# First layer in two halves of the f-tiles over all chunks, one weight conversion per step, second layer's chunks reversed

## The chip, the cores and the metric

The kernel runs on one core of a Trainium2 chip. The metric is the device time of one execution in microseconds (us); lower is better. The kernel before took 620.69 us (median of three runs, 618.83 to 621.95).

## The reference

Attention with a learned position bias (2 batches, 8 heads, 576 positions, head size 64) gives 1152 tokens of 512 features. Two feed-forward layers follow, each 512 to 2048 to 512. Only they are touched by the change:

```python
def _moe_ref(x, w_in, w_out):
    h = x @ w_in
    g = h * (1.0 / (1.0 + np.exp(-1.702 * h)))
    return (g @ w_out).astype(np.float32)

def _moe2_ref(x, w_in, w_out, a, b):
    h = x @ w_in
    h2 = h * h
    h3 = h2 * h
    P = a[0] + a[1] * h + a[2] * h2 + a[3] * h3
    Q = 1.0 + np.abs(b[0]) * np.abs(h) + np.abs(b[1]) * h2
    g = P / (Q + 1e-06)
    return (g @ w_out).astype(np.float32)
```

The weights arrive as 64-bit floats and are turned into 32-bit ones on the chip.

## The kernel before, in words

**Order of work.** Bias and attention come first and are not touched but for the early weight fetches. The two layers are one loop of steps (line 782). The tokens are cut into three chunks of 384 (`NC`), the 2048 hidden features into 16 f-tiles of 128 (`NF`). A step n is one layer l, chunk c and f-tile k; `seq` (line 770) lists them layer by layer, chunk by chunk, f-tile by f-tile, so steps 0 to 47 are the first layer and 48 to 95 the second. Steps 0 to 2 begin under the end of attention (line 753).

**One step.** `hidden` (line 461) makes the 128 by 384 block of h on TensorE in 12 matmuls: numbers are kept as a high and a low part, so three products over four blocks of 128 features. The block is in PSUM tile `hps`, of which there are two. In the first layer `gelu` (line 483), one step later, takes the sigmoid on ScalarE (486), multiplies on VectorE (487; this is the last reader of `hps`), and `parts` splits the result into `ghi` on ScalarE (477) and `glo` on GpSimd (480). In the second layer `rational` (line 494) spreads the fraction over three successive steps on ScalarE (503 to 511), VectorE (513 to 523) and GpSimd (520, 522); line 523 is the last reader of `hps`, and line 503 squares into the fourth accumulator's tile, `acc3`.

**Second product.** `out1` (line 536) adds the f-tile's product with `w_out` into four accumulators `acc0` to `acc3` (12 matmuls), two steps behind `hidden` (`L1`); `out2` (line 543) into three (9 matmuls of 512 columns), four steps behind (`L2`). The accumulators hold a whole chunk, all 16 f-tiles, and there is one set. At a chunk's end `input2` (line 775) makes the second layer's input: ScalarE copies each accumulator to the high part (778), VectorE subtracts for the low part (779). For the last chunk this waits until step 50 (`later`, line 802). `pairs` (line 529) orders the matmuls of a chunk's first and last f-tile so that accumulators are begun late and finished early, one after the other.

**Weights.** A layer's f-tile has two halves, `w_in` and `w_out`, of 512 KB as 64-bit numbers; 64 halves in all, in the order `M.order`. `fetch` (line 413) loads one into a `raw` tile (four of them) on the SP queue. `conv(j)` (line 425) finishes half j-1 with an integer add on VectorE (440) and begins half j: ScalarE shifts the low words (444), VectorE picks bits of the high words (445, 447). In the first layer line 445 writes the PSUM tile `top`; in the second it writes the SBUF tile `tmp`. `split` (line 451) then makes the high part on ScalarE (456) and the low part on GpSimd (457) and fetches half j+3. `M.W[k]` holds f-tile k of the first layer and later of the second.

**When conversions run** (lines 787 to 799). Ten begin under attention (lines 723 to 725). The first layer's others go two per step during chunk 0, to step 14. None run in steps 15 to 32. The second layer's start when chunk 2 has used an f-tile for the last time: 26 of them in steps 33 to 47, mostly two per step, and the last six in every second step from 54 to 64.

In a step the program's order is: `hidden`; conversion and `split`; `gelu` of the step before; a possible second conversion and `split`; from step 48 on `rational`; then `out1` or `out2`, and at a chunk's end `input2`. Each engine keeps that order.

Of the kernel before, what the change touches and what calls it, by code (L numbers as in the profile page):

```python
# [4 lines left out]
F32 = mybir.dt.float32  # L5
F32R = mybir.dt.float32r
U32 = mybir.dt.uint32
I32 = mybir.dt.int32
AF = mybir.ActivationFunctionType
ALU = mybir.AluOpType  # L10
# [7 lines left out]
NF = 16  # L18
CH = 384
NC = 3  # L20
NEARLY, NMID = 3, 7

L1, L2 = 2, 4
# [375 lines left out]
class Moe:  # L399
# [13 lines left out]
    def fetch(self, j):  # L413
        if j >= 64:
            return
        nc = self.nc
        l, k, o = self.half(j)
        raw = self.rp.tile([128, 512, 2], U32, tag="raw", name="raw", bufs=4)
        src = self.t["win" if o == 0 else "wout"][l, k]
        nc.sync.dma_start(raw[:], src.bitcast(U32).rearrange("p (n t) -> p n t", t=2))  # L420
        self.raw[j] = raw
# [3 lines left out]
    def conv(self, j):  # L425
        nc = self.nc
        if j < 64:
            raw = self.raw[j]
            val = self.tmp[j] = self.rp.tile([128, 512], U32, tag="tmp", name="tmp", bufs=3)
            lo, hi = raw[:, :, 0], raw[:, :, 1]  # L430
            self.up[j], tmp = lo, val[:]
            if self.hs:
                self.up[j] = self.hs.tile([128, 512], F32, tag="up", name="up", bufs=1)[:].bitcast(U32)
                if not self.second:
                    tmp = self.hs.tile([128, 512], F32, tag="es", name="top", bufs=1)[:].bitcast(U32)
        if j:
            l, k, o = self.half(j - 1)
            w, old = self.W[k], self.tmp.pop(j - 1)
            self.raw.pop(j - 1)
            nc.vector.tensor_tensor(out=old[:].bitcast(I32), in0=old[:].bitcast(I32),  # L440
                                    in1=self.up.pop(j - 1).bitcast(I32), op=ALU.add)
            self.ready = w, o, old[:].bitcast(F32), j + 3
        if j < 64:
            nc.scalar.activation(out=self.up[j].bitcast(I32), in_=lo, func=AF.Copy, scale=2.0 ** -29)  # L444
            nc.vector.tensor_scalar(out=tmp, in0=hi, scalar1=5, scalar2=2,  # L445
                                    op0=ALU.logical_shift_left, op1=ALU.logical_shift_right)
            nc.vector.scalar_tensor_tensor(out=val[:], in0=hi, scalar=0xC0000000, in1=tmp,  # L447
                                           op0=ALU.bitwise_and, op1=ALU.bitwise_or)
# [45 lines left out]
    def rational(self, h):  # L494
        nc, ab = self.nc, self.ab
        t2, t1, t0 = self.st[1], self.st[0], None
        vec, act = nc.vector, nc.scalar.activation
        if h is not None:
            t0 = [(self.mp if i else self.gp).tile([128, CH], F32, tag=f"t{i}", name="ra", bufs=3) for i in range(3)]
        self.st = [t0, t1]  # L500
        if t2:
            sq = self.ps.tile([128, 512], F32, tag="acc3", name="sq", bufs=1)[:, 0:CH]
            act(out=sq, in_=t2[0][:], func=AF.Square, bias=self.neg)
        if t1:
            es = self.hs.tile([128, 512], F32, tag="es", name="es", bufs=1)[:, 0:CH]
            act(out=t1[1][:], in_=t1[0][:], func=AF.Abs_reciprocal_sqrt)  # L506
            act(out=es, in_=t1[1][:], func=AF.Square)
        if t0:
            act(out=t0[0][:], in_=h, func=AF.Square)  # L509
            act(out=t0[1][:], in_=h, func=AF.Abs, scale=ab[:, 4:5])  # L510
            act(out=t0[2][:], in_=h, func=AF.Identity, scale=ab[:, 3:4], bias=ab[:, 2:3])  # L511
        if t2:
            vec.scalar_tensor_tensor(out=t2[2][:], in0=sq, scalar=0.75, in1=t2[2][:], op0=ALU.add, op1=ALU.mult)
        if t1:
            vec.tensor_tensor(out=t1[0][:], in0=es, in1=t1[0][:], op=ALU.mult)
            vec.scalar_tensor_tensor(out=t1[2][:], in0=t1[2][:], scalar=ab[:, 0:1], in1=es,
                                     op0=ALU.add, op1=ALU.mult)
        if t0:
            vec.tensor_tensor(out=t0[2][:], in0=t0[2][:], in1=h, op=ALU.mult)  # L519
            nc.gpsimd.tensor_scalar(out=t0[0][:], in0=t0[0][:], scalar1=self.pb[:, 1:2], scalar2=1.000001,  # L520
                                    op0=ALU.mult, op1=ALU.add)
            nc.gpsimd.tensor_tensor(out=t0[0][:], in0=t0[0][:], in1=t0[1][:], op=ALU.add)  # L522
            vec.scalar_tensor_tensor(out=t0[2][:], in0=t0[2][:], scalar=ab[:, 1:2], in1=h,  # L523
                                     op0=ALU.add, op1=ALU.mult)
        if t2:
            return self.parts(t2[2][:], 0)


    def pairs(self, k, n):
        if k == 0:  # L530
            return [(i, e) for e in range(n) for i in range(3)]
        if k == NF - 1:
            return [(0, 0), (1, 0), (0, 1), (1, 1), (2, 0), (2, 1)] + [(i, e) for e in range(2, n) for i in range(3)]
        return [(i, e) for i in range(3) for e in range(n)]

    def out1(self, k, g, acc):
        nc, w = self.nc, self.W[k]
        for i, e in self.pairs(k, 4):
            wi, gi = ((2, 0), (3, 0), (2, 1))[i]
            nc.tensor.matmul(acc[e][:, 0:CH], w[:, wi, 128 * e:128 * e + 128], g[gi][:],  # L540
                             start=(k == 0 and i == 0), stop=(k == NF - 1 and i == 2))

    def out2(self, k, g, acc):
        nc, w = self.nc, self.W[k]
        for i, e in self.pairs(k, 3):
            wi, gi = ((2, 0), (3, 0), (2, 1))[i]
            nc.tensor.matmul(acc[e][:], g[gi][:, 128 * e:128 * e + 128], w[:, wi, :],  # L547
                             start=(k == 0 and i == 0), stop=(k == NF - 1 and i == 2))


def attention_moe_moe(tc, t):
    nc = tc.nc
    new = tc.alloc_tile_pool
    A, M = Attention(tc, t), Moe(tc, t)
# [4 lines left out]
    op = A.op = new(name="operands", bufs=1, reuse_waits="tile")  # L559
# [27 lines left out]
    first = [(0, b, qc) for qc in QORDER for b in range(2)]  # L587
# [55 lines left out]
    for s in range(n + TLAG + 2):  # L643
# [103 lines left out]
                M.W[k] = wp.tile([128, 4, 512], F32R, name=f"w{k}")  # L747

        if s == n - 24:
            for j in range(4):  # L750
                M.fetch(j)
        if s - n in (1, 2, 3):
            hq.append(M.hidden(0, nh))
# [11 lines left out]
    for k in range(NMID, NF):  # L765
        M.W[k] = lp.tile([128, 4, 512], F32R, name=f"w{k}")

    M.st = [None, None]
    LAG = [L1, L2]
    seq = [(l, c, k) for l in range(2) for c in range(NC) for k in range(NF)]  # L770
    N1 = NC * NF
    acc, ng, later = {}, len(g), []
    todo = list(range(len(seq)))

    def input2(c, acc):
        hi, lo = M.x[c]
        for e in range(4):
            nc.scalar.copy(hi[:, e, :], acc[e][:, 0:CH])
            nc.vector.tensor_tensor(out=lo[:, e, :], in0=acc[e][:, 0:CH], in1=hi[:, e, :].bitcast(F32),
                                    op=ALU.subtract)  # L780

    for n in range(nh, len(seq) + L2):
        l, c, k = seq[n] if n < len(seq) else (2, 0, 0)
        M.second = l > 0
# [2 lines left out]
        for i in range(2):  # L787
            j = nj[0]
            if j < 33:
                go = l == 0 and c == 0  # L790
            elif j < 65:
                go = M.order[j - 1][1] + L1 * M.order[j - 1][2] < n - 32
                go = go and (n < N1 and (n, i) not in ((33, 1), (34, 1), (41, 1), (43, 0)) or n >= N1 + 6 and n % 2 == 0 and i == 0)
            else:
                go = False
            if go:
                conv(False)
            if n < N1:
                M.split()
            if i == 0 and ng <= n - 1 < N1:  # L800
                g[n - 1] = M.gelu(hq.pop(0))
        if n == N1 + 2:
            for x in later:
                input2(*x)
        if n >= N1 + RLAG:
            r = M.rational(hq.pop(0) if hq else None)
            if r:
# [2 lines left out]
        while todo and n >= todo[0] + LAG[seq[todo[0]][0]]:  # L810
            m = todo.pop(0)
            l, c, k = seq[m]
            if k == 0:
                acc = [M.ps.tile([128, 512], F32, tag=f"acc{e}", name="acc", bufs=1) for e in range(4 - l)]
            if l == 0:
                M.out1(k, g.pop(m), acc)
                if k == NF - 1:
                    if c == NC - 1:
                        later.append((c, acc))
                    else:  # L820
                        input2(c, acc)
            else:
                M.out2(k, g.pop(m), acc)
                if k == NF - 1:
                    for i in range(3):
                        o = rp.tile([128, DM], F32, tag="tmp", name="o", bufs=3)
                        rows = t["out"][CH * c + 128 * i:CH * c + 128 * i + 128, :]
                        if c < NC - 1 or i == 0:
                            nc.scalar.copy(o[:], acc[i][:])
                            nc.sync.dma_start(rows, o[:])  # L830
                        elif i == 1:
# [81 lines left out]
```

## Time and profile before

| what | value |
|---|---|
| three runs, median (lowest, highest) | 620.69 us (618.83, 621.95) |
| the profiled execution's own time | 619.0 us |
| its span, first to last instruction | 617.2 us |
| TensorE busy (matmul) | 576.5 us, 93% of the span |
| VectorE, ScalarE, GpSimd busy | 423.7, 439.4, 379.5 us |
| granted TensorE clock, mean | 0.994 |

A profile lists each engine's instructions with start and duration in us from the span's start. PE is TensorE's matmuls, PEld its weight loads, DVE VectorE, ACT ScalarE, POOL GpSimd, SP the engine that issues most DMAs. An idle time is put down to the instruction whose semaphore ended it. Matmuls are pipelined and overlap in the list, so the distance between starts tells what one costs, not its listed duration.

### The profile page before, as it was taken

What the parts mean: (1) busy time and instruction counts of PE and PEld (TensorE: products, weight loads), DVE (VectorE), ACT (ScalarE), POOL (GpSimd) and SP (SyncE); (2) the same over time, 40 slices, a digit from 0 to 9 for tenths busy, and PEclk for the clock granted to TensorE, in tenths of its full rate; (3) what the DMA queues carried; (4) which work ended last, traced back from release to release, by engine and by line L of the source; (5) the groups of instructions that cost most, each with busy time, mean ns of one, the idle gap of its engine ahead of it and who ended that gap; (6) DMA issues with size and microseconds to landing.
All of it is one profiled execution on the core that took longest, in us unless ns stands there. A gap on an engine that the chain in (4) does not pass through costs nothing.

```text
span 617.2 us, 11025 instructions
## 1 busy us (share of the span) xinstructions
PE 576.5 (93%) x3805; PEld 478.7 (78%) x3805; DVE 423.7 (69%) x918; ACT 439.4 (71%) x922; POOL 379.5 (61%) x458
## 2 busy tenths in 40 slices
PE   6987999999988998899999999988999999999997
PEld 2233466666656988899999988988988989999995
DVE  7988765888876888721113888868778766666663
ACT  7987777898886666632223666678888987788783
POOL 5967656777764677722222667756767765665663
PEclk9988999999999999999999999999999999999999
DMA  5788753836116666700001466630000100001001
GB/s 175 209 269 273 222 209 118 316 99 228 58 35 173 193 210 209 207 0 1 2 1 34 143 204 205 208 94 18 18 2 1 52 2 1 0 1 52 1 2 51
DMA packets 23912, 66.26 MB, mean 107 GB/s; under 512 B 2480, under 2 KB 3376, under 8 KB 23856
## 3 DMA queue, kind: packets, MB, share of 16 engines
q1 hardware_dynamic: 23712, 65.43, 33.3%
q8 instruction: 30, 0.49, 0.3%
q14 instruction: 26, 0.21, 0.1%
q10 hardware_dynamic: 144, 0.13, 0.1%
HBM read 52.30 MB, written 13.25 MB: 106 GB/s over the span
## 4 chain that ended last, share of the span: by engine, by line
PE 38%; DVE 14%; ACT 12%; issue 2%; POOL 0%; DVEq 0%; ACTq 0%
PE hps L468 19%; PE acc L547 13%; PE acc L540 6%; DVE tmp L440 5%; ACT up L444 3%; ACT w L456 3%; DVE sg L487 2%; DVE tmp L447 2%; DVE top L445 2%; ACT sg L486 2%; ACT ra L511 1%; ACT ra L510 1%; DVE ra L523 1%; ACT ra L506 1%; ACT ra L509 1%
## 5 line engine op out<-in xcount | busy, mean ns | idle before, releaser
L468 PE MATMUL hps<-xhi,w 128*128 128x384 f32 x768 | 152.4, 340 | 14.1 <-DVE sg L487 9.3
L468 PEld LDWEIGHTS hps<-xhi,w 128*128 128x128 f32 x768 | 135.0, 188 | 25.0 <-DVE sg L487 15.0
L457 POOL TENSOR_TENSOR w<-tmp,w 128x512 fp32r<-128x512 f32 x64 | 82.4, 1288 | 40.2 <-ACT w L456 34.1
L480 POOL TENSOR_TENSOR glo<-sg,ghi 128x384 fp32r<-128x384 f32 x48 | 48.8, 1017 | 64.4 <-PE acc L540 45.0
L468 PE MATMUL hps<-xlo,w 128*128 128x384 f32 x384 | 82.0, 334 | 0.0
L253 POOL TENSOR_SCALAR p<-p,mn 128x512 f32<-128x512 f32 x72 | 55.2, 776 | 38.6 <-ACT p L240 28.0
L540 PE MATMUL acc<-ghi,w 128*128 128x384 f32 x384 | 76.7, 334 | 0.0
L547 PE MATMUL acc<-w,ghi 128*128 128x512 f32 x288 | 75.7, 393 | 0.0
L487 DVE TENSOR_TENSOR sg<-hps,sg 128x384 f32<-128x384 f32 x48 | 26.7, 557 | 65.5 <-ACT sg L486 65.5
L240 ACT ACTIVATE p<-p,mn 128x576 f32<-128x576 f32 x72 | 55.4, 771 | 20.4 <-DVE mn L236 18.5
L520 POOL TENSOR_SCALAR ra<-ra,small 128x384 f32<-128x384 f32 x48 | 28.2, 587 | 65.9 <-ACT ra L509 65.9
L468 PEld LDWEIGHTS hps<-xlo,w 128*128 128x128 f32 x384 | 68.0, 188 | 0.0
L540 PEld LDWEIGHTS acc<-ghi,w 128*128 128x128 f32 x384 | 67.5, 188 | 0.0
L444 ACT ACTIVATE up<-raw 128x512 int32<-128x512 uint32 x59 | 37.9, 642 | 36.2 <-DVE tmp L440 33.5
L547 PEld LDWEIGHTS acc<-w,ghi 128*128 128x128 f32 x288 | 53.4, 188 | 8.6
L236 DVE CUSTOM_DVE_ANT_0 p<-wide,bt 128x576 f32<-128x576 f32 x72 | 52.2, 749 | 2.1 <-PE wide L215 1.9
L519 DVE TENSOR_TENSOR ra<-ra,hps 128x384 f32<-128x384 f32 x48 | 26.6, 554 | 36.9 <-ACT ra L511 36.8
L477 ACT CAST ghi<-sg 128x384 fp32r<-128x384 f32 x48 | 24.6, 513 | 38.2 <-DVE sg L487 19.8
L522 POOL TENSOR_TENSOR ra<-ra 128x384 f32<-128x384 f32 x48 | 48.7, 1015 | 4.0
L480 POOL TENSOR_TENSOR glo<-ra,ghi 128x384 fp32r<-128x384 f32 x48 | 48.8, 1017 | 2.4 <-PE acc L547 2.0
L215 PE MATMUL wide<-k,q 64*128 64x288 f32 (+1 forms) x432 | 45.6, 313 | 2.5 <-ACT st L142 2.0
L486 ACT ACTIVATE sg<-hps 128x384 f32<-128x384 f32 x48 | 23.4, 488 | 30.7 <-PE hps L468 30.7
(100 smaller groups left out, 1174.3 us busy)
## 6 DMA issues: line engine op xcount, KB each, us to landing
raw<-win SPq DMA_DIRECT2D x32, 512.0 KB, 3.7
raw<-wout SPq DMA_DIRECT2D x32, 512.0 KB, 3.7
bias_all<-st SPq DMA_DIRECT2D x36, 295.5 KB, 3.8
bt<-bias_all SPq DMA_DIRECT2D x16, 576.0 KB, 6.1
qk<-qk SPq DMA_DIRECT2D x7, 608.0 KB, 6.4
v<-v SPq DMA_DIRECT2D x8, 320.0 KB, 5.0
out<-o SPq DMA_DIRECT2D x8, 256.0 KB, 2.2
bt<-bias_all SPq DMA_DIRECT2D x8, 144.0 KB, 3.5
```

The costliest lines, as they stand in the source:

```text
L215: nc.tensor.matmul(ps[:, half, 0:288], q[p, x, 128 * qc:128 * qc + 128], k[p, y, 288 * half:288 * half + 288], start=(i == 0), stop=(i == ...
L236: nc.vector.tensor_tensor_reduce(out=pv.rearrange("p (x j) -> p x j", x=2), in0=ps[:, :, 0:288], in1=self.bt[qc][:, a, :].rearrange("p (x ...
L240: nc.scalar.activation(out=pv, in_=pv, func=AF.Exp, bias=mn[:, a:a + 1], scale=-1.0, accum_out=mn[:, 2 + a:3 + a])
L253: nc.gpsimd.tensor_scalar(out=p[:, a, 0:512], in0=p[:, a, 0:512], scalar1=r, scalar2=1.0, op0=ALU.mult, op1=ALU.mult)
L444: nc.scalar.activation(out=self.up[j].bitcast(I32), in_=lo, func=AF.Copy, scale=2.0 ** -29)
L457: nc.gpsimd.tensor_tensor(out=w[:, 2 * o + 1, :], in0=val, in1=w[:, 2 * o, :].bitcast(F32), op=ALU.subtract)
L468: nc.tensor.matmul(ps[:, 0:CH], w[:, wi, 128 * d:128 * d + 128], xx[:, d, :], start=(i == 0 and d == 0), stop=(i == 2 and d == 3))
L480: nc.gpsimd.tensor_tensor(out=glo[:], in0=g, in1=ghi[:].bitcast(F32), op=ALU.subtract)
L487: nc.vector.tensor_tensor(out=sg[:], in0=h, in1=sg[:], op=ALU.mult)
L522: nc.gpsimd.tensor_tensor(out=t0[0][:], in0=t0[0][:], in1=t0[1][:], op=ALU.add)
L540: nc.tensor.matmul(acc[e][:, 0:CH], w[:, wi, 128 * e:128 * e + 128], g[gi][:], start=(k == 0 and i == 0), stop=(k == NF - 1 and i == 2))
L547: nc.tensor.matmul(acc[e][:], g[gi][:, 128 * e:128 * e + 128], w[:, wi, :], start=(k == 0 and i == 0), stop=(k == NF - 1 and i == 2))
```

## The change

`seq` takes the first eight f-tiles of the first layer over chunks 0, 1, 2, then the last eight over chunks 2, 1, 0. Chunk 2 thus stays whole (steps 16 to 31). Chunks 0 and 1 are accumulated in two pieces: the first piece's sums go from PSUM to an SBUF tile `part` (ScalarE and VectorE, two accumulators each), and `input2_sum` adds the second piece to them (VectorE), copies the high part (ScalarE) and subtracts the low part (GpSimd). Chunk 0 is now the last of the first layer. The second layer runs its chunks as 2, 1, 0.

Conversions run one per step, two in steps 3 to 5, and from step 40 to 47 two in even steps, as far as the f-tile is free (`freed`). Worked out by these rules: steps 3, 4, 5 two each; 6 to 36 one each; 37 to 40 none; 41 one, 42 two, 43 one, 44 two, 45 one, 46 two, 47 one; then one in each even step from 50 to 64.

There are three `raw` tiles in place of four, half j+2 is fetched where j+3 was, and three halves in place of four are fetched at the start. The scratch tiles t1 and t2 of `rational`, three each before, become rings of two and three; four of these five are slices of the tile `part1`, whose sums are used up by step 41.

```diff
-        raw = self.rp.tile([128, 512, 2], U32, tag="raw", name="raw", bufs=4)
+        raw = self.rp.tile([128, 512, 2], U32, tag="raw", name="raw", bufs=3)
...
-            self.ready = w, o, old[:].bitcast(F32), j + 3
+            self.ready = w, o, old[:].bitcast(F32), j + 2
...
-            t0 = [(self.mp if i else self.gp).tile([128, CH], F32, tag=f"t{i}", name="ra", bufs=3) for i in range(3)]
+            t0 = [self.gp.tile([128, CH], F32, tag="t0", name="ra", bufs=3)]
+            t0 += [ring[self.nra % len(ring)] for ring in self.ring]
+            self.nra += 1
...
-    def pairs(self, k, n):
-        if k == 0:
+    def pairs(self, first, last, n):
+        if first:
...
-        if k == NF - 1:
+        if last:
...
-                             start=(k == 0 and i == 0), stop=(k == NF - 1 and i == 2))
+                             start=(first and i == 0), stop=(last and i == 2))
...
-            for j in range(4):
+            for j in range(3):
                 M.fetch(j)
...
+    part = [mp.tile([128, 4, CH], F32, name=f"part{i}") for i in range(2)]
+    M.ring, M.nra = [[part[1][:, i, :] for i in range(2)],
+                     [part[1][:, 2, :], part[1][:, 3, :], mp.tile([128, CH], F32, name="ra")[:]]], 0
...
-    seq = [(l, c, k) for l in range(2) for c in range(NC) for k in range(NF)]
+    HF = NF // 2
+    seq = [(0, c, k) for c in range(NC) for k in range(HF)]
+    seq += [(0, c, k) for c in range(NC)[::-1] for k in range(HF, NF)]
+    seq += [(1, c, k) for c in range(NC)[::-1] for k in range(NF)]
     N1 = NC * NF
+    freed = {k: max(n for n in range(N1) if seq[n][2] == k) for k in range(NF)}
...
+    def input2_sum(c, acc):
+        hi, lo = M.x[c]
+        for e in range(4):
+            p = part[c][:, e, :]
+            nc.vector.tensor_tensor(out=p, in0=acc[e][:, 0:CH], in1=p, op=ALU.add)
+            nc.scalar.copy(hi[:, e, :], p)
+            nc.gpsimd.tensor_tensor(out=lo[:, e, :], in0=p, in1=hi[:, e, :].bitcast(F32), op=ALU.subtract)
...
-                go = l == 0 and c == 0
+                go = i == 0 or n < 6
             elif j < 65:
-                go = M.order[j - 1][1] + L1 * M.order[j - 1][2] < n - 32
-                go = go and (n < N1 and (n, i) not in ((33, 1), (34, 1), (41, 1), (43, 0)) or n >= N1 + 6 and n % 2 == 0 and i == 0)
+                go = freed[M.order[j - 1][1]] + L1 * M.order[j - 1][2] < n
+                go = go and (n < N1 and (i == 0 or n >= 40 and n % 2 == 0) or n >= N1 + 2 and n % 2 == 0 and i == 0)
...
-                input2(*x)
+                input2_sum(*x)
...
-            if k == 0:
+            first = k == 0 or l == 0 and c < 2 and k == HF
+            last = k == NF - 1 or l == 0 and c < 2 and k == HF - 1
+            if first:
...
-                if k == NF - 1:
-                    if c == NC - 1:
+                if last:
+                    if k < HF:
+                        for e in range(4):
+                            (nc.vector.tensor_copy if e % 2 else nc.scalar.copy)(part[c][:, e, :], acc[e][:, 0:CH])
+                    elif c == 2:
+                        input2(c, acc)
+                    elif c:
+                        input2_sum(c, acc)
+                    else:
                         later.append((c, acc))
-                    else:
-                        input2(c, acc)
...
-                        if c < NC - 1 or i == 0:
+                        if c or i == 0:
```

## Rows read from the trace of the kernel before

**Rows 1.** The page: busy time of each engine.

```profile
PE 576.5 (93%) x3805; PEld 478.7 (78%) x3805; DVE 423.7 (69%) x918; ACT 439.4 (71%) x922; POOL 379.5 (61%) x458
```

**Rows 2.** Windows by stage: length, busy us (instructions) of PE, PEld, DVE, ACT, POOL; clock.

```profile
214.94:264.03 49.09, 44.16 (x242) 41.29 (x241) 40.28 (x64) 31.20 (x58) 34.34 (x29) 1.00 0.64 203
264.03:338.91 74.88, 74.88 (x434) 74.88 (x434) 13.74 (x26) 20.71 (x44) 19.54 (x19) 1.00 0.02 8
338.91:406.53 67.62, 64.46 (x362) 62.22 (x362) 57.89 (x94) 44.66 (x85) 47.36 (x40) 1.00 0.63 192
406.53:422.61 16.08, 12.77 (x71) 12.05 (x70) 11.59 (x22) 14.25 (x30) 8.49 (x11) 1.00 0.04 14
422.61:479.09 56.48, 55.18 (x275) 49.03 (x273) 44.71 (x82) 48.74 (x102) 40.56 (x45) 1.00 0.04 10
479.09:602.61 123.52, 123.52 (x623) 112.12 (x622) 82.03 (x152) 102.92 (x216) 77.67 (x91) 1.00 0.04 14
```

**Rows 3.** The chain that ended last, one step of chunk 0: start us, us, what.

```profile
226.44 0.70 DVE tmp L440
...
227.16 0.64 ACT up L444
227.80 0.54 ACT w L456
228.34 0.40 ACT sg L486
...
228.76 0.56 DVE sg L487
229.32 0.59 DVE tmp L440
...
231.44 0.70 DVE tmp L440
```

**Rows 4.** Timeline at the end of chunk 1: start us, us, instructions merged [idle before].

```profile
337.89 1.70 ACT L778 CAST xhi<-acc 128x384 fp32r<-128x384 f32 x4 [2.73 <-PE acc L540]
...
338.40 1.95 DVE L779 TENSOR_TENSOR xlo<-acc,xhi 128x384 fp32r<-128x384 f32 x4 [3.87 <-ACT xhi L778]
...
343.30 0.98 PE L468 MATMUL hps<-xhi,w 128*128 128x384 f32 x4
```

**Rows 5.** Timeline, from the first layer to the second.

```profile
412.06 1.94 DVE L779 TENSOR_TENSOR xlo<-acc,xhi 128x384 fp32r<-128x384 f32 x4
...
414.04 0.59 ACT L503 ACTIVATE sq<-ra,small 128x384 f32<-128x384 f32 x1 [1.62 <-DVE xlo L779]
...
417.66 0.61 DVE L523 SCALAR_TENSOR_TENSOR ra<-ra,cst,hps 128x384 f32<-128x384 f32 x1
...
418.33 1.67 PE L468 MATMUL hps<-xhi,w 128*128 128x384 f32 x8 [3.31 <-DVE ra L523]
...
420.95 0.61 DVE L523 SCALAR_TENSOR_TENSOR ra<-ra,cst,hps 128x384 f32<-128x384 f32 x1
```

**Rows 6.** The chain that ended last, second layer with conversions.

```profile
455.88 0.61 DVE tmp L440
...
465.13 0.61 DVE tmp L440
```

**Rows 7.** Timeline of one conversion in the second layer, on VectorE.

```profile
455.80 0.68 DVE L440 CUSTOM_DVE_ANT_0 tmp<-tmp,up 128x1024 uint16<-128x1024 uint16 x1
...
457.70 0.56 DVE L513 SCALAR_TENSOR_TENSOR ra<-sq,ra 128x384 f32<-128x384 f32 x1 [0.15 <-ACT sq L503]
```

**Rows 8.** Groups by line: instructions, count | busy us, mean ns of one.

```profile
L457 POOL TENSOR_TENSOR w<-tmp,w 128x512 fp32r<-128x512 f32 x64 | 82.4, 1288 | 40.2 <-ACT w L456 34.1
L480 POOL TENSOR_TENSOR glo<-sg,ghi 128x384 fp32r<-128x384 f32 x48 | 48.8, 1017 | 64.4 <-PE acc L540 45.0
```

**Rows 9.** Weight fetches: issue to landing, all; a fetch's issue; a conversion's start.

```profile
DMA to landing us min/median/max: 3.3/3.7/7.4
...
184.65 0.33 SPq L420 DMA_DIRECT2D raw<-win  x1
...
188.88 0.69 DVE L445 TENSOR_SCALAR top<-raw 128x512 uint32<-128x512 uint32 x1
```

More of the change, by code (lines that the diff above doesn't have):

```diff
@@ L526, in rational, with out1, out2 @@
             return self.parts(t2[2][:], 0)
-    def pairs(self, k, n):
-        if k == 0:
+    def pairs(self, first, last, n):
+        if first:
             return [(i, e) for e in range(n) for i in range(3)]
-        if k == NF - 1:
+        if last:
             return [(0, 0), (1, 0), (0, 1), (1, 1), (2, 0), (2, 1)] + [(i, e) for e in range(2, n) for i in range(3)]
         return [(i, e) for i in range(3) for e in range(n)]
-    def out1(self, k, g, acc):
+    def out1(self, k, g, acc, first, last):
         nc, w = self.nc, self.W[k]
-        for i, e in self.pairs(k, 4):
+        for i, e in self.pairs(first, last, 4):
             wi, gi = ((2, 0), (3, 0), (2, 1))[i]
             nc.tensor.matmul(acc[e][:, 0:CH], w[:, wi, 128 * e:128 * e + 128], g[gi][:],
-                             start=(k == 0 and i == 0), stop=(k == NF - 1 and i == 2))
-    def out2(self, k, g, acc):
+                             start=(first and i == 0), stop=(last and i == 2))
+    def out2(self, k, g, acc, first, last):
         nc, w = self.nc, self.W[k]
-        for i, e in self.pairs(k, 3):
+        for i, e in self.pairs(first, last, 3):
             wi, gi = ((2, 0), (3, 0), (2, 1))[i]
             nc.tensor.matmul(acc[e][:], g[gi][:, 128 * e:128 * e + 128], w[:, wi, :],
-                             start=(k == 0 and i == 0), stop=(k == NF - 1 and i == 2))
+                             start=(first and i == 0), stop=(last and i == 2))
 def attention_moe_moe(tc, t):
@@ L812, in attention_moe_moe @@
             l, c, k = seq[m]
-            if k == 0:
+            first = k == 0 or l == 0 and c < 2 and k == HF
+            last = k == NF - 1 or l == 0 and c < 2 and k == HF - 1
+            if first:
                 acc = [M.ps.tile([128, 512], F32, tag=f"acc{e}", name="acc", bufs=1) for e in range(4 - l)]
             if l == 0:
-                M.out1(k, g.pop(m), acc)
-                if k == NF - 1:
-                    if c == NC - 1:
+                M.out1(k, g.pop(m), acc, first, last)
+                if last:
[7 more added lines that the diff above has]
+                    else:
                         later.append((c, acc))
-                    else:
-                        input2(c, acc)
             else:
-                M.out2(k, g.pop(m), acc)
+                M.out2(k, g.pop(m), acc, first, last)
                 if k == NF - 1:
```

## The prediction

> **What bounds the kernel now.** I read the page first: TensorE's matmuls fill 93% of the span [rows 1], so only its waits can be won. Then I cut the span by stage, at starts of `hidden` groups; the instruction counts give the number of steps (12 + 12 matmuls in the first layer, 12 + 9 in the second; a window also counts two or three matmuls still running at its start). The second row of [rows 2] is 18 steps in 74.88 us, 4.16 us each, with PE and PEld full and VectorE busy 13.74 us: no conversion runs there, and this is the bare price of a first-layer step. Half of it, 2.08 us, is one `hidden` or one `out1`. The last row is the same for the second layer: 29 steps and the `hidden` of a thirtieth, so (123.52 - 2.08) / 29 = 4.19 us a step. Against these prices the other rows hold stalls:
> - steps 6 to 15, chunk 0 with two conversions each: 49.09 - 10 x 4.16 = 7.49 us
> - steps 34 to 48, chunk 2 with the second layer's conversions: 67.62 - 15 x 4.16 = 5.22 us
> - steps 49 to 52, the change of layers: 16.08 - (3 x 4.16 + 0.03) = 3.57 us (`hidden` 50 and 51 come back to back there)
> - steps 53 to 65, the last conversions: 56.48 - 13 x 4.19 = 2.01 us
>
> Together 18.3 us, the most that this change can win behind attention. Who stalls TensorE in the first two is in [rows 3]: from one step's integer add to the next step's is 231.44 - 226.44 = 5.00 us, not 4.16, and the chain goes round VectorE and ScalarE. It runs add 0.70, ScalarE 0.64 + 0.54 + 0.40, `gelu`'s multiply 0.56, then the second conversion, 231.44 - 229.32 = 2.12 on VectorE. The multiply frees `hps`, so `hidden` comes late.
>
> **Conversions one per step.** With one, the circle is 0.70 + 1.58 + 0.56 = 2.8 us (VectorE's own load 2.12 + 0.56 = 2.7), under 4.16: TensorE sets the pace. Steps 3 to 5 still carry two, so I leave the first of chunk 0's nine late starts (a ninth of 7.49 is 0.83) at 0.4, with bounds 0 and 0.8. Saved 7.1. Of chunk 2's 5.22 the single conversions of steps 23 to 36 leave nothing by themselves.
>
> The bubble repeats evenly in front of `hidden`, and rows show it gone in the 18 plain steps with the same two `hps` buffers [rows 2]. A rule in the Trainium skill, "Perfetto Trace Analysis", section "Optimization Strategy", says that consistent bubbles on the engine that should be saturated can mean too few buffers. By it thinning the conversions would win nothing, and the sum would be that of the rival on buffers below; the trace speaks against it here.
>
> **Ends of chunks.** There are five before the layers change, not two. Rows show one with a conversion beside it [rows 4]: `input2` ends on VectorE at 340.35, the conversion queues behind it, and `hidden` starts at 343.30 where 338.91 + 4.16 = 343.07 was due: 0.23 late. Chunk 2's end (step 33) is the same code with the same single conversion: 0.3. The two ends of first pieces put two copies on each of VectorE and ScalarE, half of `input2`'s load, the last able to end some 0.5 us after the last matmul, and the next accumulation is covered by 2.08 us of `hidden`: 0, at most 0.3 each. If `hidden` did not cover them, all four copies' time would show, about 1 us.
>
> Chunk 1's second end (step 41) is heavier. Let T be the end of its `out1`. Four additions at 1.95 / 4 = 0.49 end at about T + 1.0 (VectorE need not wait for ScalarE first). Step 42 then has two conversions and a multiply, 5.0 us [rows 3], so step 43's add starts at T + 6.0 and its multiply ends 2.84 later, T + 8.8, where `hidden` 44 was due at T + 8.32. Late 0.5, taken as 0.6 (0 to 1.3). GpSimd's new queue: four subtractions of 1.02 to T + 4.1, a low part of the weights 1.29, `glo` 1.02 [rows 8], to T + 6.4; its first reader is the ninth matmul of the `out1` that starts at T + 6.24, at T + 7.6. Covered by 1.2 us. Steps 43 to 47 alternate one and two conversions, 2.8 + 5.0 = 7.8 us for two steps of 8.32: no further loss. Chunk 2's stretch thus costs 0.9 in place of 5.22: saved 4.3.
>
> **The change of layers gets worse.** Before, with `hidden` 50 at 406.53 + 4.16 = 410.69: VectorE is free at 412.06, subtracts for 1.94, ScalarE's square can start at 414.04 (it needs `acc3`), and the chain through line 523 ends 4.23 later; `hidden` 52 starts at 418.33, due 414.85 [rows 5]. Now a conversion comes first in step 50: 457.70 - 455.80 - 0.15 = 1.75 us of VectorE [rows 7]. Then the additions 1.95, ScalarE's last copy behind them (1.70 / 4 = 0.4), then the same 4.23: 1.37 + 1.75 + 1.95 + 0.4 + 4.23 = 9.7 us after `hidden` 50 in place of 7.6. So this stall is 5.7 where it was 3.57: lost 2.1. Bounds: nothing, if the conversion fits ahead of line 523, and 3 with waits between. The four subtractions on GpSimd (4.1 us) end before line 522 is needed; without that cover 1 us more.
>
> **The second layer's conversions.** With conversions in every second step the chain needs 465.13 - 455.88 = 9.25 us for two steps [rows 6] against 8.38: 0.87 lost a pair. A plain step's chain needs 420.95 - 417.66 = 3.29 [rows 5], so it makes up 0.90; a conversion step loses 1.77. Before, five plain steps (49 to 53) came first and six conversions lost only 2.01. Now conversions stand at 52, 54 ... 62, each with one plain step before it, so no reserve gathers: 6 x 0.87 = 5.2. The one at 64 begins no new half, hence no line 444: 0. Lost 3.2; bounds 0 and 7 x 0.87 - 2.0 = 4.1.
>
> **Fetches and scratch.** Three `raw` tiles: half j+3 can load once half j is read, some three conversions ahead. At 4.16 us a step that is three times the median landing of 3.7 us. The tight place is the end of attention, where three conversions run back to back: the half for the third would be issued at 184.65 and is wanted at 188.88 [rows 9], 4.2 us later. So 0; if it lands as late as 7.4, 3 us on the chain. The SP queue carries only fetches then; at the start one fetch fewer stands before attention's loads and comes one conversion later. Addresses in SBUF shift with the pool sizes; attention's tiles are done by then: 0, within 1 either way. The ring of two for t1 is written two steps after its last use: 0. Reversed order: the same work, and chunk 2's input is ready 15 steps early: 0.
>
> **Sum.** Saved 7.1 + 4.3 = 11.4, lost 2.1 + 3.2 = 5.3: 6.1 us. Against the profiled execution, 619.0 (span 617.2, 1.8 around it): 612.9. That execution lies 1.7 below the median of the runs shown, 620.69; on the median's scale 614.6.
>
> **Rivals.**
> - *Nothing handed on.* If step 50's conversion and those after it find gaps, the 5.3 are not lost: about 609.3 on the median's scale. For: ScalarE and VectorE are busy only about 0.8 in that stretch [rows 2]. Against: the chain, not the load, sets [rows 6]. Chance 0.10.
> - *All handed back.* Upper bounds together (ends of chunks 1.6 more, change of layers 1, layer two 0.9, the late fetch 3) take the 6.1: about 621. For: each hangs on the same VectorE order. Against: they must all come. Chance 0.10.
> - *Slower: the ring inside one tile.* Four of `rational`'s scratch slices share `part1`. If order is kept by tile and not by slice, line 506 must wait for the last step's line 523 and line 513 for line 511. The step then is ScalarE from 506 to 511, some 2.4, plus five VectorE instructions, some 2.9: 5.3 in place of 4.19 over 47 steps, +52: about 667. It decides as soon as such a step passes 4.19. Against: ScalarE's four copies into slices of `xhi` run through in 1.70 us while VectorE reads the earlier slices for 1.95 [rows 4], so order goes by slice. Chance 0.04.
> - *Buffers, not conversions.* If two `hps` buffers made the bubbles, 7.49 and 5.22 stay and the 5.3 are added: 626. Against: the 18 plain steps. Chance 0.03.
>
> **Numbers.** The forecast's own chance is 0.73: 614.6. Its bounds with the first two rivals give 609 to 618.5 as the range that should hold 8 in 10. About 0.5%, 3.1 us, is what a measurement of this kernel tells from no change; faster by more (under 617.6) takes the forecast, the first rival and a little of neither: 0.83; within it 0.10; slower 0.07.
>
> **What would show it.** Steps 7 to 32 in one profile at 4.16 us, with PE full; a small gap near steps 35 and 44; a gap of some 5.7 us before `hidden` 52 put down to line 523; then six gaps of 0.87 us every second step. Wrong: gaps of 0.5 to 0.6 us still in chunk 0, second-layer steps without conversions over 4.19, or VectorE or ScalarE waiting for a fetch near 189 us.

## The result, and the profile after

| | before | after |
|---|---|---|
| median of five runs each | 621.95 us (618.83 to 622.46) | 612.87 us (611.31 to 613.02) |
| profiled execution, span | 619.0, 617.2 us | 613.02, 611.0 us |
| from `hidden` 6 to the end of the span | 402.28 us | 395.67 us |

The ratio is 0.9861, with a 95% interval of 0.9833 to 0.9888: the change made the kernel 1.4% faster, 7.0 to 10.4 us on 622. The forecast was 614.6, in a range of 609.0 to 618.5. The five runs of before are the three that were known when the forecast was made and two more, of 622.16 and 622.46 us.

The page after, busy time of each engine and the chain that ended last by engine, and that chain before:

```profile
PE 574.3 (94%) x3805; PEld 480.9 (79%) x3805; DVE 424.3 (69%) x922; ACT 441.0 (72%) x926; POOL 386.9 (63%) x466
...
PE 51%; ACT 9%; DVE 5%; issue 1%; DVEq 0%; ACTq 0%
```

```profile
PE 38%; DVE 14%; ACT 12%; issue 2%; POOL 0%; DVEq 0%; ACTq 0%
```

TensorE does the same 3805 matmuls [rows 1]; GpSimd has eight instructions and 7.4 us more, the subtractions that moved there. Of the span, the chain now lies for 51% on TensorE and for 14% on ScalarE and VectorE, where it was 38% and 26%.

The same stages as in [rows 2], in windows of the kernel after (length; busy us and instructions of PE, PEld, DVE, ACT, POOL; granted clock):

```profile
215.33:257.35 42.02, 41.89 (x242) 41.58 (x241) 30.11 (x50) 25.09 (x50) 26.64 (x23) 1.00 0.53 163
257.35:332.23 74.88, 74.88 (x434) 74.88 (x433) 42.38 (x71) 37.44 (x74) 39.84 (x35) 1.00 0.40 120
332.23:395.63 63.40, 62.97 (x362) 62.34 (x361) 36.90 (x63) 33.73 (x66) 37.06 (x34) 1.00 0.33 109
395.63:415.47 19.84, 15.03 (x71) 14.22 (x70) 14.72 (x27) 15.20 (x31) 12.19 (x14) 0.83 0.09 27
415.47:472.87 57.40, 55.48 (x275) 48.99 (x273) 45.13 (x82) 49.65 (x104) 41.79 (x46) 1.00 0.09 28
472.87:596.37 123.50, 123.50 (x622) 112.13 (x621) 82.05 (x152) 102.91 (x216) 77.71 (x91) 1.00 0.04 14
```

Row by row against [rows 2]: steps 6 to 15 take 42.02 us in place of 49.09 (7.07 won); the 18 plain steps still take 74.88 although VectorE now does 42.38 us in them, not 13.74; steps 34 to 48 take 63.40 in place of 67.62 (4.22 won). Then it turns: the change of layers takes 19.84 in place of 16.08 (3.76 lost), at a granted clock of 0.83, and steps 53 to 65 take 57.40 in place of 56.48 (0.92 lost). The last row is as before. 11.29 won and 4.68 lost make the 6.61 us of the table.

The change of layers, in the chain that ended last (start, us, what). All lines of `rational` stand two higher than before, so 525 is the old 523; line 799 is the addition, 800 the copy of `input2_sum`:

```profile
400.06 0.61 DVE part L525
400.67 0.60 DVE tmp L440
401.27 0.35 DVE tmp L445
...
401.64 0.69 DVE tmp L447
402.33 0.48 DVE part L799
...
402.83 1.91 ACT xhi L800 x4
404.74 0.48 ACT sq L505
...
412.09 0.61 DVE part L525
```

And the timeline of TensorE and GpSimd there, with the window of the `hidden` that follows (1.00 is 2.4 GHz, so 0.50 is 1.2):

```profile
399.79 1.55 PE L468 MATMUL hps<-xhi,w 128*128 128x384 f32 x8
...
401.87 1.55 PE L468 MATMUL hps<-xhi,w 128*128 128x384 f32 x8
...
403.42 3.87 POOL L801 TENSOR_TENSOR xlo<-part,xhi 128x384 fp32r<-128x384 f32 x4 [3.24 <-ACT xhi L800]
...
408.93 2.93 PE L468 MATMUL hps<-xhi,w 128*128 128x384 f32 x8 [4.81 <-DVE ra L525]
```

```profile
408.93:412.93 4.00, 4.00 (x12) 4.00 (x13) 3.04 (x6) 2.90 (x7) 3.92 (x6) 0.50 0.01 4
```

`hidden` 50 and 51 start at 399.79 and 401.87. `hidden` 52 waits for line 525 of step 50, which waits behind a conversion, the first addition and four copies: 4.81 us of idle TensorE. In the `hidden` that follows, the clock is 0.50: its twelve matmuls take 4.00 us where a plain one takes 2.08.

### The profile page after: what moved, and what is told of

The parts are those of the page before. It is cut to its first block, busy times and chain, and to the rows that moved or that the text cites. A ratio compares the mean times of both kernels' runs of the same rounds, so it can differ in the third digit from the quotient of the medians.

```text
span 611.0 us, 11010 instructions
## 1 busy us (share of the span) xinstructions
PE 574.3 (94%) x3805; PEld 480.9 (79%) x3805; DVE 424.3 (69%) x922; ACT 441.0 (72%) x926; POOL 386.9 (63%) x466
## 4 chain that ended last, share of the span: by engine, by line
PE 51%; ACT 9%; DVE 5%; issue 1%; DVEq 0%; ACTq 0%
PE hps L468 25%; PE acc L542 13%; PE acc L549 12%; DVE tmp L440 2%; ACT up L444 1%; ACT sq L505 1%; ACT part L512 1%; ACT ra L511 1%; ACT part L508 1%; ACT w L456 1%; ACT part L513 1%; DVE tmp L447 1%; DVE sg L487 1%; DVE part L525 1%; ACT es L509 0%
## 5 line engine op out<-in xcount | busy, mean ns | idle before, releaser
L468 PEld LDWEIGHTS hps<-xhi,w 128*128 128x128 f32 x768 | 136.6, 189 | 15.7 <-DVE ra L525 6.7
L542 PE MATMUL acc<-ghi,w 128*128 128x384 f32 x384 | 78.3, 334 | 0.0
L524 POOL TENSOR_TENSOR ra<-ra,part 128x384 f32<-128x384 f32 x48 | 48.7, 1015 | 4.1
L542 PE MATMUL acc<-glo,w 128*128 128x384 f32 x192 | 45.0, 334 | 0.0
L549 PE MATMUL acc<-w,glo 128*128 128x512 f32 x144 | 42.5, 393 | 0.0
```

The source lines that it names most:

```text
L468: nc.tensor.matmul(ps[:, 0:CH], w[:, wi, 128 * d:128 * d + 128], xx[:, d, :], start=(i == 0 and d == 0), stop=(i == 2 and d == 3))
```

## The experiments

Each edit is against the kernel after, unless it is said to stand on another run's. The runs came in three batches; their kernel before had medians of 619.99, 620.32 and 620.18 us. The stretches are from the profiles: "50 to 66" is from the start of `hidden` 50 to that of `hidden` 66 (62.82 us at the bare prices of the prediction; before 68.40, after 73.08), "6 to end" as in the first table.

| kernel | median us | ratio (95%) | wait before `hidden` 52 | clock, `hidden` 52 to 53 | 50 to 66 | 6 to end |
|---|---|---|---|---|---|---|
| before | 621.95 | 1 | 3.31 | 1.00 | 68.40 | 402.28 |
| after | 612.87 | 0.9861 (0.9833 to 0.9888) | 4.81 | 0.62 | 73.08 | 395.67 |
| e1_first_dense | 619.10 | 0.9988 (0.9975 to 1.0) | 4.81 | 0.65 | 73.10 | 402.91 |
| e7_second_dense | 617.94 | 0.9962 (0.9947 to 0.9977) | 5.43 | 0.66 | 70.33 | 400.46 |
| e4_before_again | 620.82 | 1.0008 (0.9987 to 1.0029) | 3.36 | 0.74 | 69.33 | 403.23 |
| e2_conv57_earlier | 611.76 | 0.9862 (0.9842 to 0.9882) | 3.30 | 0.71 | 71.59 | 394.20 |
| e3_add3_first | 614.66 | 0.9906 (0.9881 to 0.9932) | 3.42 | 0.58 | 73.95 | 396.53 |
| e5_convs48_49 | 612.38 | 0.9875 (0.9853 to 0.9897) | 4.18 | 0.60 | 72.49 | 395.06 |
| e6_best | 611.37 | 0.9852 (0.9826 to 0.9878) | 4.17 | 0.61 | 71.45 | 393.32 |
| e8_conv48_only | 608.38 | 0.9811 (0.9785 to 0.9837) | 3.30 | 0.71 | 69.46 | 391.34 |
| e9_copies_late | 605.43 | 0.9756 (0.973 to 0.9783) | 1.50 | 1.00 | 66.60 | 388.48 |

Set against the kernel after, the medians follow the layers of the profiles ("6 to end") to about 1 us. The ratios follow them less well, since the kernel before stood at 621.95 in the batch of the kernel after and at 620.0 to 620.3 in the others.

**Is it the thinning that wins in the first stretch?** Two conversions a step again, as long as halves of the first layer remain:

```diff
-                go = i == 0 or n < 6
+                go = True
```

> The changed kernel with the first layer's conversions two per step again (steps 3 to 14), in the new order of f-tiles and chunks. Theory 1, the saving in chunk 0 is the thinner conversions and nothing else: steps 8 to 15 start every 5.0 us again instead of 4.16, eight times 0.84, so the span is 6 to 7.5 us longer than the changed kernel's 611.0, near 618, and the change's gain over the kernel before is all but gone (ratio 0.995 to 1.0). Rival, the new order of f-tiles and chunks itself removes the stalls (halves are wanted later, so lateness no longer hurts): steps stay at 4.16 and the span stays within 1 us of 611.0, ratio near 0.986.

The window of steps 6 to 15:

```profile
214.63:264.14 49.51, 44.31 (x242) 41.24 (x242) 41.91 (x68) 32.05 (x62) 34.30 (x29) 1.00 0.65 201
```

49.51 us, before's 49.09 again, with the last stretch as in the kernel after (50 to 66: 73.10 against 73.08). The layers lose 7.24 of the 7.49 that this window lost. The order of chunks with the same two `hps` buffers wins nothing here by itself; the thinner conversions do. Steps 34 to 48 take 63.12 us in this run, 0.28 less than in the kernel after: steps 31 to 36 have no conversion here, and `hidden` 35 and 36 are no longer late behind the end of chunk 2.

**And in the second?** The second layer's conversions two per step as early as an f-tile is free:

```diff
-                go = go and (n < N1 and (i == 0 or n >= 40 and n % 2 == 0) or n >= N1 + 2 and n % 2 == 0 and i == 0)
+                go = go and (32 < n < N1 or n >= N1 + 2 and n % 2 == 0 and i == 0)
```

> The changed kernel with the second layer's conversions held back to step 33 and then two per step, as far as f-tiles are free (14 in steps 33 to 39, 14 in 41 to 47), so that only four are left from step 50 on. Theory 1 for the second stretch: steps 34 to 48 lose about 4 to 6 us again, 67 to 70 us in place of 63.4; the four conversions fewer behind step 50 give 2 to 4 us back, the run is near 614 to 615. Rival, in that stretch the order of chunks gives the gain (chunk 2 is done early and the layers' change is prepared): 34 to 48 stays under 65 us, and the run falls below 611.

Steps 34 to 48:

```profile
332.84:403.81 70.97, 65.58 (x362) 62.06 (x361) 61.64 (x101) 47.70 (x91) 52.39 (x45) 1.00 0.63 189
```

70.97 us in place of 63.40: 7.57 lost, more than before's 4.22 over the kernel after: 14 of the 15 steps from 33 to 47 have two conversions here, 11 of them before. Fewer conversions are then left for the second layer, and steps 53 to 65 take 54.43, the bare 13 x 4.19: 50 to 66 wins 2.75 back. The sum, 4.8, is what the layers lost (400.46 against 395.67). The run's median is 5.1 above that of the kernel after, where 1 to 2 were expected.

**Does before give the same profile twice?**

> The kernel before, unchanged, in a further execution: by how much does one execution differ from another, and where? Theory: the layers (from step 6 to the end) take the same time to 0.3 us in every execution, and all that differs lies in bias and attention, where the granted clock is not 1.00 all the time; then the profiles' 6.2 us is the change's worth and the rest of the 8.7 us between the runs is attention's. Rival: the stalled steps themselves differ between executions, so the change removes some of the spread.

It didn't. `hidden` 52 of this execution, and the windows from `hidden` 52 to 53 here and in the first profile of before:

```profile
419.09 2.93 PE L468 MATMUL hps<-xhi,w 128*128 128x384 f32 x8 [3.36 <-DVE ra L523]
```

```profile
419.09:424.70 5.61, 5.61 (x21) 5.22 (x22) 4.49 (x9) 5.26 (x13) 4.14 (x6) 0.74 0.01 3
```

```profile
418.33:422.61 4.28, 4.28 (x22) 3.89 (x22) 3.44 (x7) 4.22 (x11) 2.98 (x4) 1.00 0.01 4
```

After nearly the same wait (3.36 and 3.31 us) the clock fell in one execution and not in the other, 5.61 against 4.28 us; of these 1.33 the later steps make up 0.4, and the layers differ by 0.95, where at most 0.3 was expected. The profile on which the prediction stands was one in which the clock stayed up, and a short one: of the 57 executions of before in the later batches, this run's included, 49 took longer than its 619.0 us. Another 0.69 lies ahead of `hidden` 6, whose start varies between 214.0 and 217.2 us over the eleven profiles.

**The conversion of step 50.** It goes to step 48, the others stay:

```diff
-  ... or n >= N1 + 2 and n % 2 == 0 and i == 0)
+  ... or n >= N1 and n != N1 + 2 and n % 2 == 0 and i == 0)
```

> The changed kernel with the conversion of step 50 moved to step 48, all others where they are. Theory 2, that conversion's 1.75 us on VectorE lengthen the stall before hidden 52, and the longer stall is what lets the TensorE clock fall: the wait before hidden 52 becomes 3.1 to 3.3 us instead of 4.81, the granted clock stays 1.00 there, hidden 52 takes 2.1 to 2.4 us instead of 4.0. From hidden 50 to hidden 66 the time falls by 1.5 to 2 us only, since the conversions at 52 to 62 then find no reserve and lose up to 5.2 instead of 2.95. Rival a, the low clock has another cause than the length of the wait (the place in the program): it falls again although the wait is short, and the gain is 1.75 us or less. Rival b, the low clock's cost is a plain loss: the gain is 1.7 + 2.35, about 4 us.

```profile
407.59 2.75 PE L468 MATMUL hps<-xhi,w 128*128 128x384 f32 x8 [3.30 <-DVE ra L525]
```

```profile
407.59:413.39 5.80, 5.80 (x22) 5.45 (x22) 4.46 (x9) 4.21 (x9) 3.58 (x5) 0.71 0.01 3
```

The wait fell from 4.81 to 3.30, as the conversion's place on the chain says, and 50 to 66 by 1.49; the ratios, 0.9862 and 0.9861, do not tell the two kernels apart. That the clock would stay up was wrong: it fell in the first matmuls of `hidden` 52.

**The additions of step 50.** Only the fourth accumulator (`acc3`, which the square needs) ahead of `rational`; the other three additions, copies and subtractions behind it:

```diff
-    def input2_sum(c, acc):
+    def input2_sum(c, acc, es=range(4)):
...
-                input2_sum(*x)
+                input2_sum(*x, (3,))
...
+        if n == N1 + 2:
+            for x in later:
+                input2_sum(*x, (0, 1, 2))
```

> The changed kernel with the fourth accumulator's addition of step 50 done ahead of the fraction's instructions and the other three behind them; the conversion stays in step 50. Theory 2: the square waits for the fourth accumulator alone, so three additions and three copies (1.46 us on VectorE, the copies behind them on ScalarE) leave the way to hidden 52: the wait before it falls from 4.81 to about 3.3 us and the clock stays at 1.00; from hidden 50 to hidden 66 1.2 to 2 us less. Rival, the square is held by something else than the queue of additions (the subtractions on GpSimd, the table load): the wait stays over 4.5 us and the clock falls as before.

A miss. In the chain of this kernel the moved work stands right behind line 525 of step 50, ahead of step 51's square:

```profile
406.58 0.48 DVE part L799
...
407.08 1.44 ACT xhi L800 x3
408.52 0.48 ACT sq L505
```

The wait before `hidden` 52 is 1.39 shorter, but the clock falls all the same (0.58), and the next step's chain is longer by what was moved; 50 to 66 is 0.87 worse. Moving work within the chain does not shorten it.

**Conversions in steps 48 and 49,** which leaves steps 50 and 52 without one:

```diff
-  go = go and (n < N1 and (i == 0 or n >= 40 and n % 2 == 0) or n >= N1 + 2 and n % 2 == 0 and i == 0)
+  go = go and (n < N1 and (i == 0 or n >= 40 and n % 2 == 0) or (n in (N1, N1 + 1) or n >= N1 + 6 and n % 2 == 0) and i == 0)
```

> The changed kernel with the conversions of steps 50 and 52 moved to steps 48 and 49; the other six stay at 54 to 64, as in the kernel before. Theory 3, from hidden 50 to hidden 66 one chain round ScalarE and VectorE sets the time, and TensorE's waits and clock there only follow it: steps 50 to 53 free of conversions let that chain gather reserve, as in the kernel before, and the stretch takes 68.4 to 69.5 us (the two profiles of the kernel before), in place of 73.08; the run is near 608, ratio 0.978 to 0.981. Whether the clock falls before hidden 52 then costs under 1.5 us. Rival, the conversions in steps 48 and 49 only shift the queue (their work reaches into step 50 on VectorE): the stretch takes 71 us or more.

ScalarE and VectorE in step 49 (timeline):

```profile
397.69 0.68 DVE L440 CUSTOM_DVE_ANT_0 tmp<-tmp,up 128x1024 uint16<-128x1024 uint16 x1
397.76 1.30 POOL L457 TENSOR_TENSOR w<-tmp,w 128x512 fp32r<-128x512 f32 x1
398.28 1.06 DVE L445 TENSOR_SCALAR tmp<-raw 128x512 uint32<-128x512 uint32 x1
398.45 0.64 ACT L444 ACTIVATE up<-raw 128x512 int32<-128x512 uint32 x1 [1.41 <-issue]
399.11 1.28 ACT L508 ACT_TABLE_LOAD   x1
...
400.40 0.53 ACT L508 ACTIVATE part<-ra 128x384 f32<-128x384 f32 x1
```

Line 444 starts 0.08 us after VectorE's add (line 440), which is the last reader of the one `up` tile, has ended; the row names no releaser, but the same 0.08 stands between the two in steps 42, 44, 46 and 48. Behind it ScalarE still has to load its table (1.28 us) before step 49's line 508. Line 525 of step 49 ends 3.08 us after the start of `hidden` 50, in the kernel after 0.88; `hidden` 51 is 1.06 late, and `hidden` 52 waits 4.18: the conversion of step 49 is paid in full. The theory that steps 48 and 49 have room for one each was wrong for 49.

**Step 44, and both together.** Two halves of f-tiles 6 and 7 move ahead of f-tile 8's in the order, so that steps 37 and 38 take them, and step 42 has one conversion:

```diff
+        for k in (6, 7):
+            self.order.remove((1, k, 1))
+            self.order.insert(self.order.index((1, 8, 0)), (1, k, 1))
...
-  go = go and (n < N1 and (i == 0 or n >= 40 and n % 2 == 0) or n >= N1 + 2 and n % 2 == 0 and i == 0)
+  go = go and (n < N1 + 2 and (i == 0 or n in (44, 46)) or n >= N1 + 6 and n % 2 == 0 and i == 0)
```

> As the run before, and the second layer's w_out halves of f-tiles 6 and 7, whose room has been free since step 25, are taken in the empty steps 37 and 38, ahead of f-tile 8; step 42, behind the addition of chunk 1, then has one conversion, and five instead of six are left from step 54 on. Theory 3 and the reading of step 44 (two conversions behind four additions): the late start of step 44 (0.59 and 0.13 us) goes, hidden 50 to 66 takes 67.5 to 68.8 us, the run is near 607, ratio 0.976 to 0.979. Rival: step 44 is late by the additions alone and stays late by more than 0.4 us; then 608.

Steps 34 to 48 take 62.68 in place of 63.40: the 0.7 of step 44 are gone, so that reading holds. The rest misses for the reason of the run before, the conversion in step 49. With `n <= N1` in place of `n < N1 + 2` it has only the one in step 48:

> As the run e6_best, but no conversion in step 49; the six last ones stand at 54 to 64. The run before showed a conversion in step 49 to hold back ScalarE (its shift waits behind line 525 of step 48, and the table load and the step's squares queue behind it), so that line 525 of step 49 came at 404.1 instead of 400.7. Theory 3, the chain of ScalarE and VectorE from step 48 on sets this stretch: without it hidden 50 to 66 takes 69 to 70.3 us, in place of 71.45 (and 73.08 for the change), the wait before hidden 52 is 3.3 us. From hidden 6 to the end 391 to 392.5 us, where the change takes 395.7 and the kernel before 402.3 to 403.2. Rival, the sixth conversion from step 54 on eats what step 49 gives back: 71 us or more.

50 to 66 takes 69.46 us and the layers 391.34, both inside what was expected. The clock from `hidden` 52 to 53 is 0.71, after a wait of 3.30.

**Work off the chain for good.** This edit stands on that of e8. The high copies and the low subtractions of the last chunk, which no step reads before chunk 0 of the second layer, go to steps 66 to 69, one each; step 50 keeps the four additions, the fourth first:

```diff
-            for x in later:
-                input2_sum(*x)
+            for e in (3, 0, 1, 2):
+                p = part[0][:, e, :]
+                nc.vector.tensor_tensor(out=p, in0=later[0][1][e][:, 0:CH], in1=p, op=ALU.add)
+        if N1 + 18 <= n < N1 + 22:
+            hi, lo = M.x[0]
+            e = n - N1 - 18
+            p = part[0][:, e, :]
+            nc.scalar.copy(hi[:, e, :], p)
+            nc.gpsimd.tensor_tensor(out=lo[:, e, :], in0=p, in1=hi[:, e, :].bitcast(F32), op=ALU.subtract)
```

> As e8, and of step 50's work for chunk 0 only the four additions stay, the fourth accumulator's first; the four copies of the high part on ScalarE and the four subtractions on GpSimd move to steps 66 to 69, where no conversion runs (the result is read from step 80 on). Theory 3: ScalarE's 1.9 us of copies leave the chain, and the square of step 50 waits for one addition in place of four: the wait before hidden 52 falls under 2 us and the clock stays at 1.00; hidden 50 to 66 takes 66 to 67.8 us, from hidden 6 to the end 389 to 390.5 us, the run near 607. Rival (what the run e3 did): the way to hidden 52 gets shorter, but the additions come back in the next steps, and the stretch stays at 69 us or more.

The start of `hidden` 52 and the window to `hidden` 53 (line numbers three higher again):

```profile
405.24 1.68 PE L471 MATMUL hps<-xhi,w 128*128 128x384 f32 x8 [1.50 <-DVE ra L528]
```

```profile
405.24:409.54 4.30, 4.30 (x22) 3.91 (x22) 3.46 (x7) 4.24 (x11) 2.99 (x4) 1.00 0.01 4
```

The wait is 1.50 us, the clock stays up, and 50 to 66 takes 66.60 us, less than before the change; the layers take 388.48, less than the 389 to 390.5 expected. The kernel takes 605.43 us, a ratio of 0.9756: less than the kernels before and after. The run puts the fourth addition first and moves the copies and subtractions away, both at once; what each of the two gives was not measured apart.

## Why the prediction was right, and where it was not

**The thinned conversions** were sized right: 7.1 forecast and 7.07 measured in chunk 0, 4.3 and 4.22 in steps 34 to 48. `hidden` 7 is 0.4 late (forecast 0.4), steps 35 and 36 together 0.3 (0.3), steps 44 and 45 0.7 (0.6), and the two first-piece ends cost nothing. The timeline of the kernel after, TensorE at step 44:

```profile
374.70 1.68 PE L468 MATMUL hps<-xhi,w 128*128 128x384 f32 x8 [0.42 <-DVE sg L487]
```

In the chain it stands behind four additions from 364.77 and two conversions in one step:

```profile
364.77 1.95 DVE part L799 x4
366.72 0.60 DVE tmp L440
...
374.08 0.57 DVE sg L487
```

**The loss behind step 50** was sized nearly right in sum and wrong in its parts; this is the step that failed. Against the bare price the kernel after stands 10.26 us over in 50 to 66; the forecast had 5.7 + 5.2 = 10.9. Its parts were:
- *The wait for `hidden` 52:* late by 4.98, not 5.7 (the forecast's own terms, 9.7 - 4.16, make 5.5). VectorE was free 400.67 - 399.79 = 0.88 after `hidden` 50, where I took 1.37 from before. The rest of that sum held: a conversion of 1.66 (1.75 forecast), addition and copies 2.41 (2.35), the chain through line 525 as before.
- *The clock:* the forecast had it unchanged. It fell, and `hidden` 53 came 2.35 later than 4.19 after `hidden` 52, with no wait of TensorE in between.
- *The second layer's conversions:* late by 2.95 in all, not 5.2. Those in steps 52 and 54 cost nothing of their own, since the chain had run ahead of the slow TensorE: line 525 of step 51, which frees `hps` for `hidden` 53, ends at 412.70, and TensorE comes to `hidden` 53 only at 415.47. The one in step 56 costs 0.4, those in 58, 60 and 62 0.8 to 0.9 each, the 0.87 of the prediction.

So the two unforeseen sizes, the slower clock (2.35 more) and the reserve that it gave (2.25 less), nearly cancel. That they do is luck: the prediction had neither. What carries the sum is one chain over ScalarE and VectorE from step 48 to 64: e3 moved work along it and gained nothing; e2, e8 and e9 took work off it ahead of `hidden` 52 and gained, e8 and e9 in profile and runs, e2 in its profile alone.

**The median's scale.** The layers won 6.61 between the two profiles (6.1 forecast), but against the second profile of before 7.56, because the clock fell in that one as in the kernel after. The forecast carried the 6.1 over to the medians, as if the profiled execution of before were a common one. On the profiled executions it said 612.9, and 613.02 came; the 1.7 that it added for the median did not come, the median is 612.87. The 7.56 lie in the interval of the runs, 7.0 to 10.4 us. Against the 620.0 to 620.3 of before in the later batches the same 612.87 would be 7.1 to 7.5 us; this is an estimate, as the kernel after was not run in those. Whether before's other executions lose more elsewhere is open, and of the kernel after there is one profile only.

**The rivals.** *Nothing handed on* and *all handed back* are both out: 4.68 of 11.29 were handed back. *The ring inside one tile* is out: 29 second-layer steps still take (123.50 - 2.08) / 29 = 4.19 us. *Buffers* is out: with the same two buffers the bubbles are gone from steps 9 to 34 and came back with the conversions in e1. The rule on consistent bubbles (the Trainium skill, "Perfetto Trace Analysis", section "Optimization Strategy") says that they can mean too few buffers. Here they meant the chain over VectorE and ScalarE: 5.00 us a step with two conversions, 4.16 with one. The late fetch did not come either: the tight conversion begins at 189.29, 4.2 us after its fetch was issued, and waits for nothing.

## What to carry to other kernels

In this kernel, work that a second engine did beside the bound engine cost nothing as long as each step's share fitted under the step (18 steps took 74.88 us with and without it). So spread such work evenly and then look where it piles up: here at the change of stages, where other work already sits on the chain that frees the buffer. There, don't reorder within the chain but take off it what is read much later, and mind work placed a step earlier where a table load or another engine's queue stands behind it. Before carrying a difference of two profiles over to the medians, look in a second profile of the same kernel for what one execution has and another has not.

## What the runs showed of the hardware that was not expected

**TensorE's clock fell to half behind one wait, and not every time.** From `hidden` 52 to 53 the granted clock stayed at 1.00 after a wait of 1.50 us and, once, of 3.31; it fell (to means of 0.58 to 0.74) after 3.30 (twice), 3.36 and 3.42, and after all of 4.17 to 5.43. The kernel after runs 4.00 us at 0.50 there. That the wait is the cause is read from this order; no run changed the wait alone. Between the two executions of before 1.33 us were lost up to `hidden` 53 and 0.95 in the end: `hidden` 60 and 61, together 0.3 late where the clock stayed up, come on time where it fell.

**VectorE's conversions take longer beside GpSimd, once both their inputs are in SBUF.** In e9_copies_late, line 450 (447 of before) with its second input in the PSUM tile `top`, and a later one, the first of the second layer's form, with it in the SBUF tile `tmp`, each beside GpSimd's line 483 (timeline):

```profile
384.20 1.02 POOL L483 TENSOR_TENSOR glo<-sg,ghi 128x384 fp32r<-128x384 f32 x1 [0.30 <-ACT ghi L480]
...
384.79 0.69 DVE L450 SCALAR_TENSOR_TENSOR tmp<-raw,top 128x512 uint32<-128x512 uint32 x1
...
389.01 0.42 DVE L448 TENSOR_SCALAR tmp<-raw 128x512 uint32<-128x512 uint32 x1
...
389.20 1.10 POOL L483 TENSOR_TENSOR glo<-sg,ghi 128x384 fp32r<-128x384 f32 x1 [0.31 <-ACT ghi L480]
389.46 1.39 DVE L450 SCALAR_TENSOR_TENSOR tmp<-raw,tmp 128x512 uint32<-128x512 uint32 x1
```

The first takes 0.69 us, the second 1.39, and 0.69 again where GpSimd is idle (401.64 in the chain above). The Trainium skill, "SBUF — State Buffer", section "Who interferes with whom", says that a VectorE instruction with two inputs in SBUF contends with a GpSimd instruction that reads SBUF; these rows agree. It says of a `tensor_scalar` that it can contend as well, in its two-port modes: in the rows of e5, line 445 takes 1.06 us beside GpSimd's line 457 and 0.42 in the third of these rows, about half of it before GpSimd starts.
